# w_down as twelve rows on all partitions and three more on the lower 64, loaded by eight small loads, without filler matmuls

## The chip, the cores and the metric

The kernel runs on one core of one Trainium2 chip. The metric is the device time of one execution in microseconds (us). Executions of one kernel mostly agree within about 0.2%.

## The reference, cut to what matters

One token of a decoder layer: attention over a long key and value cache, then a gated MLP.

```python
h  = x + attention(layernorm(x))            # 32 heads, 4096 cached keys and values of 128
g  = layernorm(h) @ w_gate                  # 640 -> 1728
u  = layernorm(h) @ w_up                    # 640 -> 1728
h2 = h + (gelu(g) * u) @ w_down             # 1728 -> 640
```

There is one row of x, so every weight and every cached key and value is read once: 84.23 MB. The width 1728 is 13.5 times 128, and the half is what the change is about.

## The kernel before

The caches and weights are loaded by SyncE (SP), in order, on one queue; w_down comes last. In the kernel before, w_down is cut into 27 half rows for each *pair* of partitions. Six loads bring it, each to 64 partitions, the even ones or the odd ones:

```python
PER = 2
PAIR_UNITS = PER * DF // P                       # 27 rows for two partitions
NFC = (PAIR_UNITS + 1) // 2                      # 14 columns of the hidden vector
WD = ((0, 8), (8, 11), (11, 14))
...
for i, (a, b) in enumerate(WD):
    for odd in range(PER):
        start, end_at = max(a * D, odd * HALVES), min(b * D, (NFC - 1) * D + HALVES + odd * HALVES)
        at = (PAIR_UNITS // 2) * D * odd
        load(f"wd{i}", wd_sb[odd:P:PER, start:end_at], wd_rows[:, at + start : at + end_at])
```

Because 27 is odd, two columns of the hidden vector are used by half of the partitions only; the kernel multiplies them by a mask (`parity`, `g_own`, `hid_own`). Gate and up are 20 matmuls each, y (the product with w_down) 56. Between them stand fillers, matmuls whose result nobody reads, meant to keep TensorE's clock up:

```python
def fill(n):
    for _ in range(n):
        PE.matmul(s_bank[:], lhsT=ident[:], rhs=e_t[:].rearrange("p j h -> p (j h)"), start=True, stop=True)
...
fill(2)
PE.wait_ge(S["dve"], D_H)
pe_moments(m_ps, h_col, end)
fill(1)
...
end("g", up(g_ps, wg_sb, "wg"))
fill(6)
end("u", up(u_ps, wu_sb, "wu"))
fill(2)
PE.wait_ge(S["dve"], D_HID)
for i, (a, b) in enumerate(WD):
    PE.wait_ge(S[f"wd{i}"], 16 * PER)
    ... # the y matmuls of this group of w_down
```

The softmax here doesn't subtract the row's maximum and nothing guards it: scores larger than these inputs give would overflow.

## Time and profile before

| | before |
|---|---|
| time, median of 6 runs | 205.99 us (205.65 to 206.10) |
| span of the profiled run | 204.1 us |
| bytes read, mean rate over the span | 84.23 MB, 413 GB/s |
| last w_down increment | 200.68 us |
| up matmuls | 195.51 to 197.56 us |
| hidden vector ready (`hid`) | 198.54 us |

(An increment is one count of the semaphore by which TensorE waits for a load. The trace records 16 for a load to 64 or 128 partitions; with the last one the load is complete.)

The slices of the page come first: the span in 40 equal parts, a digit for the busy share in tenths.

```profile
PE   0003404406621861066407640482166468257972
...
PEclk9999955555585585555555555558555555555698
DMA  7999999999998999999989999999999999999980
```

The row of the DMA engines is at nine tenths nearly everywhere, so the kernel is bound by DMA; TensorE has room. The chain of waits that ended last says where the end comes from (start, length, what):

```profile
175.86 24.81 DMA big<-in_B_w_down_dram
...
200.72 0.41 PE y L378 x12
...
201.15 0.33 DVE y_row L630
```

The last load was issued at 175.86 us and had landed at 200.68; the last y matmuls, the addition and the store follow. The order of time near the end shows TensorE waiting for DMA twice (start, length, engine, line, operation, then in brackets the idle time before and what ended it):

```profile
195.51 2.05 PE L401 MATMUL u<-big,hc 128*1 128x448 bf16 x20 [0.48 <-DMA big<-in_B_w_up_dram]
...
198.37 0.17 DVE L628 TENSOR_TENSOR hid<-g_sb,u_col 128x14 bf16<-128x14 f32 x1
...
199.69 0.38 PE L378 MATMUL y<-big,hid 128*1 128x160 bf16 x12 [0.34 <-DMA big<-in_B_w_down_dram]
...
200.72 0.37 PE L378 MATMUL y<-big,hid 128*1 128x160 bf16 x10 [0.65 <-DMA big<-in_B_w_down_dram]
```

The stretches of 2 us give the granted clock, the share of TensorE's full clock that it ran at: after each stretch its length, the busy times of PE, PEld, DVE, ACT and POOL, the clock, the DMA share and GB/s.

```profile
192.00:194.00 2.00, 2.00 (x18) 0.47 (x11) 0.32 (x1) 0.00 (x0) 0.00 (x0) 0.82 0.99 420
...
196.00:198.00 2.00, 1.84 (x21) 0.37 (x10) 1.17 (x6) 0.00 (x0) 0.00 (x0) 1.00 0.99 400
198.00:200.00 2.00, 1.13 (x45) 0.69 (x44) 0.51 (x3) 0.00 (x0) 0.00 (x0) 1.00 0.40 159
```

With the fillers the clock is full from 192.7 us on. The DMA share, 0.99 and then 0.40, shows that most engines have finished by about 199 us while the kernel waits until 200.68.

Besides its views, the trace holds one record for each DMA packet (start, duration, size) and one for each semaphore increment. It does not name the DMA engine, but an engine's next packet starts 4 ns before its last one ends, so the packets can be strung into 16 chains. First, a 40,960-byte row takes 1.514 us and a 32,768-byte row 1.214: 27 bytes per ns on one engine, back to back, without idle time. Second, the 16 chains do not end together. Four are late by 0.6 to 1.6 us, and three of the four have a gap where an instruction packet lies in the trace:

| instruction packet in the kernel before | its length | what the chain beside it shows |
|---|---|---|
| 8 KB at 49.90 us | 0.32 us | gap of 0.30 us to the next row, which takes 0.66 us longer than usual |
| 16 KB at 50.01 us | 1.09 us | gap of 1.07 us, then 0.47 us longer |
| 16 KB at 56.48 us | 1.10 us | gap of 1.08 us, then 0.47 us longer |
| 8 KB at 190.69 us | 0.33 us | on the same chain as the first: 0.31 and 0.66 us |

The fourth late chain started its first row 0.7 us after most of the others. That the instruction packets cause the gaps is inferred from the times: each starts about 4 ns before a row of its chain ends, as that chain's next packet would, and the gap closes as it ends, at 51.1 us for the first of 16 KB. Followed to the end by the order of rows and increments, the latest chain, 200.68 us, is that of the 16 KB packet at 56.48; the chain of the two 8 KB packets comes second, at 200.58.

### The profile page before, as it was taken

What the parts mean: (1) busy time and instruction counts of PE and PEld (TensorE: products, weight loads), DVE (VectorE), ACT (ScalarE), POOL (GpSimd) and SP (SyncE); (2) the same over time, 40 slices, a digit from 0 to 9 for tenths busy, and PEclk for the clock granted to TensorE, in tenths of its full rate; (3) what the DMA queues carried; (4) which work ended last, traced back from release to release, by engine and by line L of the source; (5) the groups of instructions that cost most, each with busy time, mean ns of one, the idle gap of its engine ahead of it and who ended that gap; (6) DMA issues with size and microseconds to landing.
All of it is one profiled execution on the core that took longest, in us unless ns stands there. A gap on an engine that the chain in (4) does not pass through costs nothing. (4 is left out here: it accounts for less than half of the span.)

```text
span 204.1 us, 4083 instructions
## 1 busy us (share of the span) xinstructions
PE 87.7 (43%) x1837; PEld 53.6 (26%) x1839; DVE 105.2 (52%) x185; ACT 4.6 (2%) x11; POOL 6.8 (3%) x12
## 2 busy tenths in 40 slices
PE   0003404406621861066407640482166468257972
PEld 0001101105311711063107310451063164046220
DVE  5003498570658278309480957065908492732360
ACT  2000100000000000000000000000000000000000
POOL 8301000000000000000000000000000000000100
PEclk9999955555585585555555555558555555555698
DMA  7999999999998999999989999999999999999980
GB/s 249 393 475 417 411 430 469 437 411 416 437 446 381 473 450 411 424 424 456 443 370 478 437 411 430 437 443 437 395 427 424 430 433 421 433 425 429 419 369 20
DMA packets 4245, 84.30 MB, mean 413 GB/s; under 512 B 528, under 2 KB 528, under 8 KB 784
## 3 DMA queue, kind: packets, MB, share of 16 engines
q1 hardware_dynamic: 4240, 84.23, 96.7%
q8 instruction: 3, 0.05, 0.1%
q14 instruction: 2, 0.02, 0.0%
HBM read 84.23 MB, written 0.00 MB: 413 GB/s over the span
## 5 line engine op out<-in xcount | busy, mean ns | idle before, releaser
L561 DVE STREAM_TRANSPOSE big<-big 128x1024 f32<-128x1024 f32 x64 | 73.8, 1211 | 6.3 <-issue 3.8
L273 PE MATMUL o<-ex,big 128*128 128x4 bf16 x1024 | 28.6, 166 | 38.7 <-PEq L173 38.7
L273 PEld LDWEIGHTS o<-ex,big 128*128 128x128 bf16 x1024 | 28.4, 104 | 39.1 <-issue 39.1
L245 PE MATMUL s<-big,q_quad 128*8 128x512 bf16 x256 | 27.9, 579 | 24.0 <-DVE big L561 24.0
L588 DVE TENSOR_TENSOR o_col<-o,rinv 128x4 bf16<-128x4 f32 x8 | 1.3, 163 | 38.9 <-PE o L273 38.9
L245 PEld LDWEIGHTS s<-big,q_quad 128*8 128x8 bf16 x256 | 7.0, 111 | 40.1 <-DVE big L561 31.9
L570 DVE STREAM_TRANSPOSE s_turned<-s 128x512 f32<-128x512 f32 x8 | 5.7, 717 | 13.5 <-PE s L245 13.5
L280 PE MATMUL a<-wo,o_row 128*1 128x160 bf16 x256 | 9.9, 333 | 2.3 <-DVE o_row L595 2.3
L573 DVE TENSOR_TENSOR ex<-e,of_head 128x512 bf16<-128x512 f32 x8 | 5.5, 692 | 6.8 <-PE e L261 6.8
L292 PE MATMUL t<-rs_cur,ones_f 128*128 128x4 f32 x16 | 4.7, 365 | 10.1 <-DVE rs_cur L581 10.1
L280 PEld LDWEIGHTS a<-wo,o_row 128*1 128x1 bf16 x256 | 7.2, 115 | 3.0 <-DVE o_row L595 3.0
L302 PE MATMUL o<-x_col,mean_f 128*128 128x10 f32 x2 | 0.6, 376 | 16.8 <-DVE x_col L210 16.8
L292 PEld LDWEIGHTS t<-rs_cur,ones_f 128*128 128x128 f32 x16 | 4.0, 312 | 11.0 <-DVE rs_cur L581 11.0
L261 PE MATMUL e<-e_part,ident 128*32 128x32 bf16 x128 | 2.5, 197 | 10.0 <-PEq L340 10.0
L445 POOL TENSOR_TENSOR hr<-hv,half_f 128x1 f32<-128x1 f32 x1 | 0.6, 554 | 172.2 <-DVE hv L219 172.2
L223 DVE CAST x_row<-x_69 128x160 f32<-128x160 bf16 x1 | 0.2, 244 | 11.6 <-DMA x_69<-in_A_x_dram 11.6
L261 PEld LDWEIGHTS e<-e_part,ident 128*32 128x32 bf16 x128 | 1.8, 106 | 16.0 <-issue 16.0
L513 ACT ACTIVATE e_part<-s_turned 128x128 bf16<-128x128 f32 x8 | 2.5, 309 | 154.1 <-DVE s_turned L570 154.1
L302 PEld LDWEIGHTS o<-x_col,mean_f 128*128 128x128 f32 x2 | 0.5, 313 | 16.8 <-DVE x_col L210 16.8
L295 PE MATMUL o<-col_of,o_spread 128*128 128x8 bf16 x8 | 1.5, 188 | 6.8 <-issue 3.3
L441 POOL MEMSET wo<- 128x5120 bf16 x1 | 4.4, 4370 | 0.0
L318 PE MATMUL g<-big,xn_bf 128*1 128x512 bf16 x20 | 2.8, 546 | 1.9 <-DVE xn_bf L230 1.9
(84 smaller groups left out, 45.7 us busy)
## 6 DMA issues: line engine op xcount, KB each, us to landing
big<-in_A_k_cache_dram SPq DMA_DIRECT2D x7, 4096.0 KB, 20.6
big<-in_A_v_cache_dram SPq DMA_DIRECT2D x6, 4096.0 KB, 17.7
big<-in_A_v_cache_dram SPq DMA_DIRECT2D x4, 2048.0 KB, 11.9
big<-in_A_wq_dram SPq DMA_DIRECT2D x1, 5120.0 KB, 15.2
wo<-in_A_wo_dram SPq DMA_DIRECT2D x4, 1280.0 KB, 15.8
big<-in_A_k_cache_dram SPq DMA_DIRECT2D x2, 2048.0 KB, 17.6
big<-in_B_w_gate_dram SPq DMA_DIRECT2D x1, 2160.0 KB, 18.5
big<-in_B_w_up_dram SPq DMA_DIRECT2D x1, 2160.0 KB, 23.2
```

Of the source, the lines that this page charges most:

```text
L245: inst = PE.matmul(s_bank[32 * r : 32 * r + 2 * QH, :], lhsT=q_quad[:, 2 * k + e, (1 - b) * QH : (3 - b) * QH], rhs=kt_at[:, k, HALF * b + ...
L261: inst = PE.matmul(to[32 * h : 32 * h + 32, r], lhsT=ident[:, 32 * r : 32 * r + 32], rhs=e_part[:, :, :, h], start=True, stop=True, tile_p ...
L273: inst = PE.matmul(o_ps, lhsT=vt[:, j, :], rhs=e_t[:, j, :], start=(j == 0), stop=(j == NB - 1))
L280: inst = PE.matmul(attn_ps[32 * r : 32 * r + 1, :], lhsT=o_row[:, j : j + 1], rhs=wo_t[:, j, r * YW : (r + 1) * YW], start=False, stop=j = ...
L292: mark("totals", PE.matmul(ps, lhsT=ones_f[:], rhs=rs_cur[:], start=True, stop=True))
L295: inst = PE.matmul(ps, lhsT=o_spread[:].rearrange("p h c -> p (h c)"), rhs=col_of[:], start=True, stop=True)
L318: inst = PE.matmul(qr_ps[b][32 * r : 32 * r + 1, :], lhsT=xn_bf[:, c : c + 1], rhs=wq_sb[:, c, :].rearrange("p (m h d) -> p m h d", h=QH, ...
L441: POOL.memset(t[:], 0.0).then_inc(S["pool"], 1)
L513: ACT.activation(e_part[:].rearrange("p b j h -> p j b h"), s_turned[:, :, 0 : 2 * QH].rearrange("p j (b h) -> p j b h", b=2), AF.Exp, sca ...
L561: DVE.transpose(to[:, c], of[:, c].rearrange("p (j k n) -> p j k n", k=2, n=HP)).then_inc(S["kt"], 1)
L570: assert dve(lambda: DVE.transpose(s_turned[:].rearrange("p j n -> p (j n)"), s_bank[:]), False) == D_SCORES[m]
L573: DVE.tensor_tensor(e_t[:], e_ps.unsqueeze(2).broadcast_to(shape), of_head[:].unsqueeze(1).broadcast_to(shape), op=ALU.mult,).then_inc(S[" ...
```

## The change

The intent: give every partition 12 whole rows of w_down and the lower 64 partitions 3 more (12 × 128 + 3 × 64 = 1728), so that the masks fall away; load the 12 rows in three loads to all 128 partitions, and the 3 more in eight loads of 8 partitions that are 4 apart; place gate and up to match; leave out the fillers. The core of the diff:

```diff
-    WD = ((0, 8), (8, 11), (11, 14))
+    FULL = 12
+    MORE = 3
+    LOW = P // 2
+    NFC = FULL + MORE
+    WD = ((0, 7), (7, 10), (10, FULL))
 ...
-    fill(2)
     PE.wait_ge(S["dve"], D_H)
     pe_moments(m_ps, h_col, end)
-    fill(1)
 ...                                    # in up(), for each of 5 steps j and 4 groups r
+                for at, n in ((0, FULL), (FULL, MORE)):
+                    if at and r >= LOW // HP:
+                        continue
+                    first = at * P + r * n * HP
+                    to = ps[32 * r : 32 * r + 1, at * HP : (at + n) * HP]
+                    inst = PE.matmul(
+                        to.rearrange("q (c i) -> q i c", c=n), lhsT=hc[:, j : j + 1],
+                        rhs=w[:, j, first : first + n * HP].rearrange("p (i c) -> p i c", c=n), ...)
 ...
     end("g", up(g_ps, wg_sb, "wg"))
-    fill(6)
     end("u", up(u_ps, wu_sb, "wu"))
-    fill(2)
 ...
+    more = B_w_down[FULL * P : DF, :].rearrange("(p c) d -> p (c d)", c=MORE)
+    for half in range(LOW // HP):
+        for i in range(4):
+            rows = slice(HP * half + i, HP * (half + 1), 4)
+            load("wd0", wd_sb[rows, FULL:NFC, :].rearrange("p c d -> p (c d)"), more[rows])
+    wd_rows = B_w_down[0 : FULL * P, :].rearrange("(p c) d -> p c d", c=FULL)
     for i, (a, b) in enumerate(WD):
-        for odd in range(PER):
-            ...
-            load(f"wd{i}", wd_sb[odd:P:PER, start:end_at], wd_rows[:, at + start : at + end_at])
+        load(f"wd{i + 1}", wd_sb[:, a:b, :], wd_rows[:, a:b, :])
```

Gate and up become 30 matmuls each, y becomes 60, and the loads of w_down eleven.

More of the change, by code (lines that the diff above doesn't have):

```diff
@@ L50 @@
     DF = 1728
-    PER = 2
-    PAIR_UNITS = PER * DF // P
-    NFC = (PAIR_UNITS + 1) // 2
-    HALVES = D // PER
+    FULL = 12
+    MORE = 3
+    LOW = P // 2
+    NFC = FULL + MORE
     COLS = NFC * HP
-    WD = ((0, 8), (8, 11), (11, 14))
-    RG = DF // YR
+    WD = ((0, 7), (7, 10), (10, FULL))
+    RG = FULL * HP
     EPS = 1e-5
@@ L83 @@
     wu_sb = part((SLOTS + 2) * TILE + W_MLP, W_MLP).rearrange("p (c f) -> p c f", c=DC)
-    wd_sb = part(0, NFC * D)
+    wd_sb = part(0, NFC * D).rearrange("p (c d) -> p c d", c=NFC)
     ident = sb("ident", [P, P], bf16)
     ones_f = sb("ones_f", [P, P])
-    parity = sb("parity", [P, PER])
     mean_f = sb("mean_f", [P, P])
@@ L121 @@
     e2 = sb("e2", [P, NFC])
-    g_own = sb("g_own", [P, PER])
     hid = sb("hid", [P, NFC], bf16)
-    hid_own = sb("hid_own", [P, PER], bf16)
     g_col = sb("g_col", [P, NFC, HP])
@@ L147 @@
     names = (
-        ["k0", "k1", "k1b", "va", "vb", "x", "wq", "wo", "wg", "wu", "wd0", "wd1", "wd2", "out"]
+        ["k0", "k1", "k1b", "va", "vb", "x", "wq", "wo", "wg", "wu", "wd0", "wd1", "wd2", "wd3", "out"]
         + ["pe", "dve", "act", "pool", "q", "r", "kt", "dve_pe", "act_pe", "y", "all"]
@@ L203 @@
         dve(lambda: DVE.reduce_sum(col_of[:], by_c.rearrange("p c j -> p j c"), AX.X), False)
-        dve(lambda: DVE.reduce_sum(parity[:], ident[:].rearrange("p (i b) -> p b i", b=PER), AX.X), False)
         dve(lambda: DVE.reduce_sum(of_head[:], by_w, AX.X), False)
@@ L363 @@
     D_T1 = D_HV + 5
-    D_HID = D_T1 + 9
-    def fill(n):
-        for _ in range(n):
-            PE.matmul(s_bank[:], lhsT=ident[:], rhs=e_t[:].rearrange("p j h -> p (j h)"), start=True, stop=True)
+    D_HID = D_T1 + 7
     end = mark_at("end")
-    fill(2)
     PE.wait_ge(S["dve"], D_H)
     pe_moments(m_ps, h_col, end)
-    fill(1)
     def y_matmul(r, at, lhsT, rhs, stop):
@@ L394, in up @@
             for r in range(YR):
-                rhs = w[:, j, r * RG : (r + 1) * RG].rearrange("p (i f) -> p i f", f=PAIR_UNITS)
-                rhs = bass.AP(
-                    tensor=rhs.tensor,
-                    offset=rhs.offset,
-                    ap=[rhs.ap[0], rhs.ap[1], [PAIR_UNITS - NFC, PER], [1, NFC]],
-                )
-                inst = PE.matmul(
-                    ps[32 * r : 32 * r + 1, :].rearrange("q (c i b) -> q i b c", c=NFC, b=PER),
-                    lhsT=hc[:, j : j + 1],
-                    rhs=rhs,
-                    start=False,
-                    stop=(j == DC - 1),
-                    skip_group_check=True,
-                    tile_position=(0, 32 * r),
-                )
+                for at, n in ((0, FULL), (FULL, MORE)):
[4 more added lines that the diff above has]
+                    inst = PE.matmul(
+                        to.rearrange("q (c i) -> q i c", c=n),
+                        lhsT=hc[:, j : j + 1],
+                        rhs=w[:, j, first : first + n * HP].rearrange("p (i c) -> p i c", c=n),
+                        start=False,
+                        stop=(j == DC - 1),
+                        skip_group_check=True,
+                        tile_position=(0, 32 * r),
+                    )
         return inst
@@ L413 @@
     end("g", up(g_ps, wg_sb, "wg"))
-    fill(6)
     end("u", up(u_ps, wu_sb, "wu"))
-    fill(2)
     PE.wait_ge(S["dve"], D_HID)
-    for i, (a, b) in enumerate(WD):
-        PE.wait_ge(S[f"wd{i}"], 16 * PER)
+    for i, (a, b) in enumerate(((FULL, NFC), *WD)):
+        PE.wait_ge(S[f"wd{i}"], 16 if i else 16 * LOW // 8)
+        rows = P if i else LOW
         for c in range(a, b):
             for r in range(YR):
-                own = c == 0 and r < YR // 2 or c == NFC - 1 and r >= YR // 2
-                lhsT = hid_own[:, c > 0 : (c > 0) + 1] if own else hid[:, c : c + 1]
-                w = wd_sb[:, c * D + r * YW : c * D + (r + 1) * YW]
-                inst = y_matmul(r, slice(0, YW), lhsT, w, c == NFC - 1)
+                w = wd_sb[0:rows, c, r * YW : (r + 1) * YW]
+                inst = y_matmul(r, slice(0, YW), hid[0:rows, c : c + 1], w, c == FULL - 1)
     end("y", inst)
@@ L501 @@
     SP.wait_ge(S["dve"], D_SCORES[NQ - SLOTS])
-    wd_rows = B_w_down.rearrange("(i b h) d -> b i (h d)", b=1, h=PAIR_UNITS)[0]
+    more = B_w_down[FULL * P : DF, :].rearrange("(p c) d -> p (c d)", c=MORE)
[4 more added lines that the diff above has]
+    wd_rows = B_w_down[0 : FULL * P, :].rearrange("(p c) d -> p c d", c=FULL)
     for i, (a, b) in enumerate(WD):
-        for odd in range(PER):
-            start, end_at = max(a * D, odd * HALVES), min(b * D, (NFC - 1) * D + HALVES + odd * HALVES)
-            at = (PAIR_UNITS // 2) * D * odd
-            load(f"wd{i}", wd_sb[odd:P:PER, start:end_at], wd_rows[:, at + start : at + end_at])
+        load(f"wd{i + 1}", wd_sb[:, a:b, :], wd_rows[:, a:b, :])
     ACT.wait_ge(S["q"], 1)
@@ L622 @@
     dve(lambda: DVE.tensor_scalar(g_sb[:], g_sb[:], hr[:], None, op0=ALU.mult))
-    ends = slice(0, NFC, NFC - 1)
-    dve(lambda: DVE.tensor_tensor(g_own[:], g_sb[:, ends], parity[:], op=ALU.mult))
     wait_pe(T["end", "u"])
     turn_rows(u_col, u_ps)
-    dve(lambda: DVE.tensor_tensor(hid_own[:], g_own[:], u_col[:, ends, 0], op=ALU.mult))
-    assert dve(lambda: DVE.tensor_tensor(hid[:], g_sb[:], u_col[:, :, 0], op=ALU.mult), False) == D_HID
+    assert dve(lambda: DVE.tensor_tensor(hid[:], g_sb[:], u_col[:, :, 0], op=ALU.mult)) == D_HID
     wait_pe(T["end", "y"])
@@ L644 @@
     POOL.sem_inc(S["all"], -1)
-    for name in [*once, "x"]:
+    for name in [*once, "x", "wd1", "wd2", "wd3"]:
         POOL.sem_inc(S[name], -16)
-    for i in range(len(WD)):
-        POOL.sem_inc(S[f"wd{i}"], -16 * PER)
+    POOL.sem_inc(S["wd0"], -16 * LOW // 8)
     ACT.wait_ge(S["out"], 16)
```

## The prediction

> **What bounds it.** DMA. The slices show the DMA engines 90% busy or more nearly throughout (84.23 MB, 413 GB/s). The chain of waits ends in w_down's landing: issued at 175.9 us, landed at 200.7, then 12 matmuls (0.41 us), the add (0.33), the store. The trace's packet records (a 40,960-byte row took 1.514 us, 27 B/ns on one engine) show engines back to back with no gap except where instruction fetches come between: packets of 8 and 16 KB at 49.9, 50.0, 56.5, 190.7 and 199.85 us; a 16 KB one set its engine back about 1.6 us. So w_down lands unevenly: 25 of the last group's 32 landed by 199.13, seven from 199.68 to 200.68. Four late engines set the end.
>
> **What the change moves.** Bytes stay. Before, each engine carried 138,240 B of w_down (5.11 us at 27 B/ns). The twelve full rows spread over 16 engines: 122,880 B each. The three extra rows go by loads of 8 partitions. [...] The trace agrees for the x load: 4 rows, 4 packets, on four engines. [...] Issue costs 0.3 to 0.6 us a load on SyncE, hidden under a 25 us deep queue.
>
> TensorE: before, fillers kept the clock full from 192.7 us on (stretches table), so the 20 up matmuls took 2.05 us where gate took 3.13 mostly at half clock, and y matmuls came each 23 ns (attention projection at half clock: 1.26 us for 32, 39 ns). After, gate and up are 30 matmuls each, about equal in columns. Without fillers the array rests 1.8 us between gate and up; I expect half clock from about 196 us: hid is ready near 199.4 instead of 198.55, and 60 y matmuls need up to 2.3 us. That ends near 201.7, against 201.13: TensorE competes with the DMA for the last wait.
>
> Third, the fetch at 199.85 came when its engine had just finished. It follows TensorE's place in its program, now 13 matmuls longer, so it should come near 199 to 199.5, that engine still carrying w_down: 1 to 1.6 us later there.
>
> **Sum.** Balance −0.6 to +0.6, clock 0 to +0.7, fetch 0 to +1.3, not additive. I expect +0.7: **206.7 us, 205.6 to 207.9**. Faster by over 2%: 0.01; within 2%: 0.95; slower: 0.04.
>
> **What would show it.** Packets of the 3,840-byte small loads on eight engines only, ending about 1.1 us after others of equal lag. The last stretch's granted clock: half in part of 196 to 201. y matmuls about 39 ns apart, and the first released by hid, not w_down. A fetch packet before w_down ends.
>
> **What would make it wrong.** [...] Gate alone may lift the clock for long enough (the query projection did at 22.0 us after 2.75 us busy), then no clock loss. [...] Small loads may pay a fixed cost each.

The cuts took out a rule for which engines a small load goes to, and a possible stall of +3 us that was not in the sum. The sum's first term, the balance, stood on the cut passage. It was an estimate: in the trace of the kernel before, the load of x, 4 rows, goes to four engines (four packets, each with one increment, where a load to 64 or 128 partitions has 16); if then a load of 8 rows goes to eight, the same for all the small loads, these carry 15,360 bytes more than before and the others 15,360 less, at the trace's 27 bytes per ns 0.57 us later or earlier. With this term the sum came to +0.7 us, so 206.7. That the engines are the same eight for all small loads had not been shown then.

## The result, and the profile after

The changed kernel took 206.66 us (median of 6 runs, 206.59 to 206.91), against 205.99 for the kernel before. The ratio is 1.0037, with a 95% interval from 1.0024 to 1.0050. (Ratios are the mean time of one kernel's fast runs over that of the other's of the same rounds, so not quite the ratio of the medians quoted.) It is 0.67 us slower: within 2%, but clear of noise. The prediction said 206.7.

The slices after:

```profile
PE   0004404415651851076408630664166576365762
...
PEclk9999955555555585555555555555555555555668
DMA  7999999999999999999999999999999999999970
```

The end of the chain of waits after:

```profile
178.83 22.67 DMA big<-in_B_w_down_dram
...
201.54 0.34 PE y L367 x8
...
201.90 0.32 DVE y_row L614
```

DMA still ends last, and it lands at 201.49 us, 0.81 us later than before. The order of time near the end:

```profile
195.67 3.58 PE L389 MATMUL u<-big,hc 128*1 128x384 bf16 x30 [1.97 <-DMA big<-in_B_w_up_dram]
...
200.02 0.18 DVE L612 TENSOR_TENSOR hid<-g_sb,u_col 128x15 bf16<-128x15 f32 x1
...
200.26 1.58 PE L367 MATMUL y<-big,hid 64*1 64x160 bf16 x60 [1.02 <-DVE hid L612]
201.53 0.10 PEld L367 LDWEIGHTS y<-big,hid 128*1 128x1 bf16 x8 [0.32 <-DMA big<-in_B_w_down_dram]
```

Up now takes 3.58 us instead of 2.05, and `hid` is ready at 200.20 instead of 198.54. The stretches give the reason:

```profile
192.00:194.00 2.00, 1.70 (x18) 0.59 (x10) 0.23 (x1) 0.00 (x0) 0.00 (x0) 0.78 0.90 363
...
196.00:198.00 2.00, 2.00 (x26) 0.94 (x20) 0.74 (x4) 0.00 (x0) 0.00 (x0) 0.58 0.96 389
198.00:200.00 2.00, 1.25 (x10) 0.37 (x4) 0.68 (x1) 0.00 (x0) 0.00 (x0) 0.57 0.36 145
200.00:202.00 2.00, 1.48 (x60) 0.91 (x60) 0.29 (x2) 0.00 (x0) 0.00 (x0) 1.00 0.08 20
```

The clock is at half from 196.3 to 199.7 us. In the trace's record of it (half until 192.89 us, full until 196.31, half until 199.72) the changes lie 3.41 us apart; the earlier ones, in both kernels, lie a multiple of that apart. So two things got worse at once, the DMA and TensorE. TensorE starts the y matmuls only at 200.26, and its weight loads have stood idle for just 0.32 us when the last increment lets the last eight go. Up and `hid` are what stands out in the profile, the late DMA what the chain names, and they end within a third of a microsecond of each other; experiments have to tell what each is worth.

The increments of the last load of w_down in the changed kernel, worked out from the trace's records, in us from the span's start:

```
5 increments    198.16 to 198.43
10 increments   199.06 to 199.82
1 increment     201.49
```

Fifteen engines had finished by 199.82; one is 1.67 us later. The eight small loads show on eight chains only: their semaphore received 64 increments from engines, eight for each of eight. The same late chain took one packet of each, and its eight increments, 195.81 to 197.12 us, are the last of all. The three other late engines took none: the last increments of up came at 194.38, 195.00, 195.16 and 195.62 us, so a late engine with small loads would have sent its eight after that, and but for those eight of one engine all had come by 195.45. The late chain with small loads is that of the 8 KB instruction packet, here at 192.90 us: not the latest of the profiled kernel before, but its second, 0.10 us behind.

### The profile page after: what moved, and what is told of

Read it like the earlier page. It is cut to its first block, busy times and chain, and to the rows that moved or that the text cites. A ratio compares the mean times of both kernels' runs of the same rounds, so it can differ in the third digit from the quotient of the medians.

```text
span 204.9 us, 4114 instructions
## 1 busy us (share of the span) xinstructions
PE 88.6 (43%) x1852; PEld 54.8 (27%) x1852; DVE 104.9 (51%) x182; ACT 4.6 (2%) x11; POOL 6.8 (3%) x12
## 5 line engine op out<-in xcount | busy, mean ns | idle before, releaser
L241 PE MATMUL s<-big,q_quad 128*8 128x512 bf16 x256 | 29.6, 609 | 23.9 <-DVE big L548 23.9
L389 PE MATMUL u<-big,hc 128*1 128x384 bf16 (+1 forms) x30 | 3.6, 652 | 2.0 <-DMA big<-in_B_w_up_dram 2.0
```

The source lines that it names most:

```text
L241: inst = PE.matmul(s_bank[32 * r : 32 * r + 2 * QH, :], lhsT=q_quad[:, 2 * k + e, (1 - b) * QH : (3 - b) * QH], rhs=kt_at[:, k, HALF * b + ...
L389: inst = PE.matmul(to.rearrange("q (c i) -> q i c", c=n), lhsT=hc[:, j : j + 1], rhs=w[:, j, first : first + n * HP].rearrange("p (i c) -> ...
```

## The experiments

Theory D: the late engine that took small loads sets the end; the change gave it more to carry. Rival T: TensorE without fillers sets the end. All kernels below gave the correct result, except e8.

| run | loads of the three extra rows | fillers | last increment, us | time, median us | ratio to before, 95% interval |
|---|---|---|---|---|---|
| the change | 8 × 8 partitions, lower half, 4 apart | no | 201.49 | 206.66 | 1.0037 (1.0024 to 1.0050) |
| e1_fill | the same | yes | 201.32 | 206.64 | 1.0034 (1.0021 to 1.0048) |
| e2_one_load | 1 × 64 partitions, lower half | no | 202.50 | 207.65 | 1.0079 (1.0066 to 1.0093) |
| e3_both | 1 × 64 partitions, lower half | yes | 202.44 | 207.43 | 1.0071 (1.0057 to 1.0085) |
| e4_before_nofill | (layout of before) | no | 200.80 | 206.17 | 1.0006 (0.9992 to 1.0020) |
| e5_even | 1 × 64 partitions, the even ones | yes | 200.82 | 205.96 | 1.0000 (0.9987 to 1.0014) |
| e6_contig | 8 × 8 partitions, lower half, neighbours | no | 201.97 | 207.32 | 1.0092 (1.0057 to 1.0128) |
| e7_double | as e1_fill, issued twice | yes | 202.53 | 207.82 | 1.0091 (1.0075 to 1.0106) |
| e8_short | (layout of before, short TensorE program) | no | 200.76 | 205.93 | 0.9996 (0.9981 to 1.0012) |
| e9_even_nofill | 1 × 64 partitions, the even ones | no | 200.75 | 206.00 | 0.9994 (0.9980 to 1.0008) |
| e10_upper | 8 × 8 partitions, upper half, 4 apart | yes | 203.24 | 208.61 | 1.0116 (1.0100 to 1.0132) |

The last increment is that of the profiled run, the time the median of 4 or 5 runs (6 for the change). Kernels e1 to e4, e5 to e8, and e9 with e10 ran on three different chips, so across the groups the ratios are compared.

### e1: the fillers back

```diff
+    fill(2)
     PE.wait_ge(S["dve"], D_H)
     pe_moments(m_ps, h_col, end)
+    fill(1)
 ...
     end("g", up(g_ps, wg_sb, "wg"))
+    fill(6)
     end("u", up(u_ps, wu_sb, "wu"))
+    fill(2)
```

> The changed kernel with the eleven filler matmuls put back (2, 1, 6, 2, in the places where the kernel before has them); its loads stay. Theory D (DMA balance): the last w_down increments still come near 201.5 us on one of the eight engines that carry the small loads, so the time stays at 206.5 to 206.8 us, although up takes 2.0 to 2.2 us instead of 3.6 and hid is ready about 1.3 us sooner. Rival T (TensorE clock): the end was set by late up and y matmuls, so it falls back to 205.8 to 206.1 us.

Measured: 206.64 us, as theory D said. In the order of time of e1, up takes 2.20 us and `hid` is 1.06 us sooner than in the changed kernel:

```profile
195.98 2.20 PE L396 MATMUL u<-big,hc 128*1 128x384 bf16 x30
...
198.96 0.18 DVE L621 TENSOR_TENSOR hid<-g_sb,u_col 128x15 bf16<-128x15 f32 x1
...
201.37 0.31 PE L374 MATMUL y<-big,hid 128*1 128x160 bf16 x8 [0.40 <-DMA big<-in_B_w_down_dram]
```

TensorE now waits 0.40 us for the last data, and nothing is won. Rival T falls: the slow up matmuls of the changed kernel were hidden behind the late engine.

### e2 and e3: one load for the three extra rows

e2 replaces the eight loads by one; e3 also has the fillers of e1.

```diff
-    for half in range(LOW // HP):
-        for i in range(4):
-            rows = slice(HP * half + i, HP * (half + 1), 4)
-            load("wd0", wd_sb[rows, FULL:NFC, :].rearrange("p c d -> p (c d)"), more[rows])
+    load("wd0", wd_sb[0:LOW, FULL:NFC, :].rearrange("p c d -> p (c d)"), more)
```

> The changed kernel with the three extra rows loaded by one DMA of 64 partitions in place of eight of 8 partitions; no fillers. All 16 engines then carry equal bytes (138,240 B of w_down, as before). Theory D: the last increment comes 0.6 us sooner, near 200.9 us, but with hid at 200.2 and y matmuls until about 201.7 TensorE now ends last, so only 0.1 to 0.3 us is gained: 206.3 to 206.6 us. Rival T: the load's form doesn't matter, 206.6 to 206.8 us. If the small loads' form alone was the cost and TensorE never mattered, 206.0 us.

> The changed kernel with one 64-partition load for the extra rows and the fillers back: both suspected causes undone, only the 12 + 3 layout left. If balance and clock together are the whole of it, the time comes back to the kernel before, 205.8 to 206.2 us, with the last increment near 200.7 to 200.9 us. If the 12 + 3 layout itself costs (30 matmuls instead of 20 for gate and up, 60 instead of 56 for y), it stays above 206.3.

Both expectations missed. Bytes were balanced over 16 engines (16 increments for the one load, where the eight have 64), yet the times rose to 207.65 and 207.43 us. The chain of e3 ends:

```profile
174.26 28.18 DMA big<-in_B_w_down_dram
202.44 0.04 issue
202.48 0.34 PE y L374 x8
```

The records of the packets tell why. Durations in ns, least, median and greatest, and for the 17,280-byte rows of gate and up the greatest only (644 is the median in all). Packets of 3,840 bytes are the extra rows and the 3-row group, those of 8,960 bytes the 7-row group:

```
               3,840 bytes        8,960 bytes        17,280 bytes
the change     149  149  161      338  338   348     1306
e3_both        149  149  448      338  426   999     1669
e5_even        149  149  161      338  340   349     1306
```

Packets that had nothing to do with the extra rows became slow while the extra rows came in: the rows of up and the 7-row group. Six rows of up took 0.94 to 1.67 us in e3; in the changed kernel one is slow, the row of 1.31 us after the 8 KB instruction packet. The last increment of up came at 196.70 us in e3, against 195.47 in e1. So the author supposed that the cause lies in which partitions the load of the extra rows writes, here the lower 64 alone. That became theory P, and the expectation had missed it.

### e4: the kernel before without its fillers

The reverse of e1's diff, on the kernel before.

> The kernel before without its fillers, nothing else changed. Theory D with T as runner-up: up takes about 3.1 to 3.6 us instead of 2.05, hid is ready near 199.9 instead of 198.55 us, the y matmuls end near 201.3 to 201.5 against 201.13: 0.1 to 0.4 us longer, 206.1 to 206.4 us. If only the DMA counts, 206.0. If the clock alone explains the whole change, 206.6.

Measured: 206.17 us; the interval of the ratio includes 1. The profiled run is the longest of the five, 206.49 us, and its chain ends on TensorE:

```profile
200.41 0.10 DVE hid L624
200.51 0.04 issue
200.56 1.17 PE y L376 x56
```

In that run the clock was full only from 199.4 us on. The other four took 206.06 to 206.18. In e2, also without fillers, it was full from 195.2 us. Without fillers it seems to depend on the run when the clock rises; there is one trace for each kernel only. In the median they are worth 0.2 us at most.

### e5: the same load, on the even partitions

As e3, but the three extra rows are on partitions 0, 2, ..., 126; the unused half of the columns stays zero. Same bytes, same number of loads.

```diff
-                    if at and r >= LOW // HP:
-                        continue
-                    first = at * P + r * n * HP
+                    step = 2 if at else 1
+                    first = at * P + r * n * HP // step
 ...
-                        to.rearrange("q (c i) -> q i c", c=n),
+                        to.rearrange("q (c i b) -> q b i c", c=n, b=step)[:, 0],
-                        rhs=w[:, j, first : first + n * HP].rearrange("p (i c) -> p i c", c=n),
+                        rhs=w[:, j, first : first + n * HP // step].rearrange("p (i c) -> p i c", c=n),
 ...
-    load("wd0", wd_sb[0:LOW, FULL:NFC, :].rearrange("p c d -> p (c d)"), more)
+    load("wd0", wd_sb[0:P:2, FULL:NFC, :].rearrange("p c d -> p (c d)"), more)
```

> As e3_both (one load of 64 partitions for the extra rows, fillers back), but the extra rows lie on the 64 even partitions instead of the lower 64, with gate and up placed to match. Same bytes, same number of loads, same 16 engines; only the partitions differ. In e3_both single 3,840-byte packets took up to 448 ns and 8,960-byte packets 426 at the median, where 149 and 338 are free. Theory P[...]: packets fall back to 149 to 165 and 338 to 360 ns, the last increment comes at 200.6 to 201.0 us instead of 202.4, time 205.8 to 206.3 us. Rival F (a 64-row load of 3,840-byte rows is slow in itself, or the 12 + 3 layout): as e3_both, 207.3 to 207.6 us.

Measured: 205.96 us, the time of the kernel before to the hundredth, and packets at 149 to 161 and 338 to 349 ns. Theory P holds and F falls: neither the layout of 12 and 3 rows nor a load of 64 rows costs anything here; which partitions it goes to decides (207.43 us for the lower 64, 205.96 for the even ones). By what mechanism it does, the trace doesn't show. The chain of e5:

```profile
174.28 26.53 DMA big<-in_B_w_down_dram
200.82 0.04 issue
200.86 0.34 PE y L374 x8
```

Against e1 the last increment came 0.50 us sooner, and the ratio fell by 0.0034. So the whole loss of the changed kernel comes back when its small loads are replaced by one load to the 64 even partitions, which has 16 increments. Number of loads, shares of the engines and partitions change together here; it takes e7 to tell that the bytes of the latest engine count.

### e6: eight small loads of neighbouring partitions

```diff
-            rows = slice(HP * half + i, HP * (half + 1), 4)
+            rows = slice(HP * half + 8 * i, HP * half + 8 * (i + 1))
```

> The changed kernel, its eight small loads of 8 partitions each taking 8 neighbouring partitions instead of 8 that are 4 apart. Same bytes on the same eight engines. Theory P: [...] the 3,840-byte packets take several times 149 ns (300 to 600), the last increment comes 1 to 3.5 us later than 201.5, time 207.5 to 210 us. Rival (spacing is without effect, only the number of engines counts): 206.5 to 206.9 us, packets at 149 ns.

Measured: 207.32 us, with runs from 207.12 to 208.98. The direction is that of theory P, the size was overestimated: 3,840-byte packets reached 278 ns (median 153), 8,960-byte packets had a median of 432 instead of 338, and the last increment came at 201.97, 0.48 us after the changed kernel's. So the spacing of 4 in the change is worth 0.7 us by the medians and 1.1 us by the ratios (0.0055 of 206; the mean of these four runs includes the one of 208.98). TensorE was through with 52 of the y matmuls at 202.00, 0.03 us after the last increment: a tie, so it adds next to nothing.

### e7: the small loads twice

```diff
             load("wd0", wd_sb[rows, FULL:NFC, :].rearrange("p c d -> p (c d)"), more[rows])
+            load("wd0", again[rows], more[rows])
```

`again` is unused space; the semaphore's counts are adapted.

> As e1_fill (changed kernel with fillers), each of the eight small loads issued a second time into unused space: 30,720 B more on each of the eight engines, nothing more on the other eight. Theory D: the late low engine is later by 30,720 B at 27 B/ns, 1.13 us[...]: last increment near 202.5 to 202.8 instead of 201.3, time 207.6 to 208.0. Rival (the total traffic of all 16 engines counts, not the fullest engine): 245,760 B at 413 GB/s, 0.6 us: 207.1 to 207.3.

("Low" is the word for the late engine that took small loads; the trace doesn't number the engines.)

Measured: 207.82 us, as theory D said; the rival's 207.1 to 207.3 is excluded. The last increment came at 202.53, that is 1.21 us after e1's, for 30,720 bytes more on each of eight engines (1.13 us at 27 bytes per ns). The other fifteen engines had finished by 201.05. What counts is the load of the latest engine, at the rate of one engine; the total doesn't. The chain of e7 ends in that load:

```profile
184.30 18.23 DMA big<-in_B_w_down_dram
202.53 0.04 issue
202.58 0.46 PE y L374 x7
```

### e8: a short program for TensorE

The kernel before without fillers, with 9 instead of 128 value matmuls per turn, half of the projection and half of the y matmuls. Its result is wrong; its loads are those of before.

```diff
-        for j in range(half * NB // 2, (half + 1) * NB // 2):
+        for j in [half * (NB - 1)] if half else range(8):
 ...
-        for j in range(HG):
+        for j in (0, 1, 2, HG - 1):
 ...
-            for r in range(YR):
+            for r in (0, YR - 1):
```

> The kernel before with TensorE's program made short on purpose (9 instead of 128 value matmuls per turn, half the projection and half the y matmuls, no fillers; its result is wrong, its loads are the same). Theory I (the late engines are late because TensorE's program is fetched through them in the middle of the kernel): the 16 KB instruction packets near 50, 56 and 200 us vanish, perhaps the 8 KB ones too; then the sixteen engines end within about 0.7 us of each other, the last increment near 199.3 to 199.8 instead of 200.7, time 204.4 to 205.0 us. If the 8 KB packets stay, one engine stays about 1.5 us late and the time is 205.6 to 206.1. Rival (lateness has another cause): packets gone but the last increment still at 200.5 or later.

Measured: 205.93 us, the expectation's middle case. Of the five instruction packets, the 16 KB ones near 56 and 200 us are gone, and with them one of the four late engines: three remain. But both 8 KB packets and the 16 KB one at 50 us stayed, and the latest of the three still ended at 200.76. So the packets near 56 and 200 us follow TensorE's program; what asks for the others is open. Theory I is borne out in part only, and gains nothing while one late engine keeps its lag.

### e9: even partitions, no fillers

The load and layout of e5, without the fillers.

> As e5_even (balanced load on the even partitions, 205.96 us) but without the fillers: the fourth corner of loads by fillers. With the DMA balanced, the last increment comes near 200.8 us again; if up runs partly at half clock (3.0 to 4.2 us) hid is ready near 199.7 to 200.4 and 60 y matmuls end near 201.3 to 201.8, so TensorE ends last by 0.2 to 0.6 us: 206.1 to 206.6 us. If the fillers are worth nothing once the DMA is balanced: 205.9 to 206.0.

Measured: 206.00 us in the median (205.88 to 206.47), as the expectation's last case. The profiled run is again the longest, and TensorE ends it:

```profile
200.10 0.20 DVE hid L608
200.30 0.04 issue
200.34 1.24 PE y L367 x60
```

In that run the clock was at half until 199.5 us. The four other runs took 205.88 to 206.16. So the fillers are no gain in the median. Whether they guard against an occasional half a microsecond isn't shown: the kernel before, with them, also had a run of 206.40 in the same rounds.

### e10: the small loads on the upper half

As e1, but partitions 64 to 127 instead of 0 to 63.

```diff
-                    if at and r >= LOW // HP:
+                    if at and r < LOW // HP:
                         continue
-                    first = at * P + r * n * HP
+                    first = at * P + (r - LOW // HP if at else r) * n * HP
 ...
-            load("wd0", wd_sb[rows, FULL:NFC, :].rearrange("p c d -> p (c d)"), more[rows])
+            load("wd0", wd_sb[LOW:P][rows, FULL:NFC, :].rearrange("p c d -> p (c d)"), more[rows])
```

> As e1_fill (eight loads of 8 partitions 4 apart, fillers back, 206.64 us), but on the upper 64 partitions instead of the lower 64. Theory K (a load of 8 partitions uses the same eight engines whatever the partitions): the small loads again go to the eight engines of which one is the latest, which is again near 201.3 us or later,[...] packets over 165 ns appear; time 206.6 to 207.6 us. Rival M (the engine follows the partition, upper partitions go to the other eight engines): the latest engine is relieved, the three other late ones get more; last increment near 200.9 to 201.1, packets at 149 ns, time 206.1 to 206.4 us.

Measured: 208.61 us, beyond the range of theory K and far from that of M. The latest engine again took the small loads, now about 0.3 us apart instead of 0.19 (by its increments), and the last increment came at 203.24. So, as far as the latest engine shows it, the engines of a load of 8 partitions don't follow the partitions. The trace doesn't number them, but had the upper half gone to the other eight, the latest engine would have been relieved. The last increment came 1.92 us after e1's. Why the upper half costs that, the trace doesn't show.

## Why the prediction was right or wrong

The time was right (206.7 predicted, 206.66 measured), and its first term carries all of it. Two of the three terms of its sum came to nothing.

- **Bound by DMA, and the end set by late engines: right.** The chain of waits ended in w_down in both kernels, and one engine was 1.67 us behind the other fifteen after the change.
- **Balance, −0.6 to +0.6: right, at the upper end.** It said 0.57 us more for an engine with small loads. On the latest engine of each run the stretch from the last increment of up to the last of w_down was 5.22 us before (195.46 to 200.68) and 5.87 after (195.62 to 201.49): 0.65 us more. (For the engine of the 8 KB packets, the second before and the latest after, it was 5.22 before too: 195.36 to 200.58.) The next late engine after the change, without small loads, needed 4.66 us (195.16 to 199.82). The estimates, 153,600 and 122,880 bytes at 27 bytes per ns, were 5.68 and 4.54. e5 gives back 0.68 us of the median (e1 to e5), and e7 shows the slope. What the prediction couldn't tell was which late engines took small loads, and so the sign: had it been none, it said itself, the change would have gained 0.5 us. It was one, the latest.
- **Clock, 0 to +0.7: the mechanism right, its share of the time nil.** Up did run at half clock (3.58 us against 2.05), `hid` came 1.66 us later. But "60 y matmuls need up to 2.3 us" was wrong: the clock was full again at 199.7 us, and TensorE was through with 52 of them and idle 0.32 us before the last data came at 201.49. e1 shows the fillers to be worth 0.02 us in the median.
- **Fetch, 0 to +1.3: this step failed.** The prediction put the last instruction packet "near 199 to 199.5, that engine still carrying w_down". It came at 201.29 us, after the last data packet of any engine (201.04). It follows TensorE's place in its program, as supposed (e8), but the y matmuls themselves came later. In e5 it came at 198.47 and delayed no increment that counted.
- **Small loads paying a fixed cost: did not happen.** Eight loads of 30 KB took 149 ns a packet; what is left beyond their bytes is at most 0.08 us for all eight (0.65 us against 0.57 here, 1.21 against 1.13 in e7).

So it is partly luck that the sum was met to 0.04 us: the +0.7 was put together from three terms of which only the first existed, and that one came out at the upper end of its range. Without e1 and e5 the clock, which is what the profile shows most plainly, would have been a wrong story.

None of the versions beats the kernel before. e5 and e9 equal it with fewer VectorE operations and no masks, e9 without fillers as well. What a faster version would have to remove is the lag of several late engines at once. About 1 us of one dates from the 8 KB packet near 190 us (0.31 us of gap and 0.66 us of a slow row in the kernel before); the cause of that packet is open. Without it alone nothing would have been won in the profiled run of the kernel before, for its engine ended at 200.58 and another, that of the 16 KB packet at 56.48 us, at 200.68.

## What to carry to other kernels

The changed kernel was bound by DMA to its end, and its time was that of the latest engine, not of the mean (in e7, against e1, 30,720 bytes more on each of eight engines ended 1.21 us later). In such a kernel count the bytes for each of the 16 engines, and look for an engine that is late already before giving some of them more. Here a load of 8 partitions put its bytes on eight engines (64 increments for the eight loads), and a load of 64 rows to the lower half of the partitions slowed other loads in flight, where the same load to every other partition didn't (207.43 against 205.96 us, e3 and e5). And before naming a slower engine as the cause, put its speed back: here the visibly slower TensorE (up in 3.58 us instead of 2.20) was fully hidden (206.66 and 206.64 us, the change and e1).
